# Convolution and two expert layers: single products in two units, and some of the tap sums moved to a DMA queue or to TensorE

## The chip, the cores and the metric

The kernel runs on one core of a Trainium2 chip. The metric is the time of one execution on the device in microseconds (us). An engine of the core has a queue of its own and works through it in order: TensorE (PE, with its weight loads as PEld), VectorE (DVE), ScalarE (ACT), GpSimd (POOL) and SyncE (SP, which only issues DMAs here). They wait for each other by semaphores.

## What is computed

`x` is 2 x 4096 x 192 and `weight_gen` 2 x 4096 x 8 x 7, all in float32. Three stages follow each other:

```python
w = exp(weight_gen - max)                      # softmax over the 7 taps of each of 8 heads
w = w / (sum(w) + 1e-9)
out[s, h, g] = sum_k w[s, h, k] * x_pad[s + k, h, g]      # causal convolution, 24 columns a head
y = square(relu(out @ w_in1)) @ w_out1         # 8192 x 192 -> 2048 -> 192
h = y @ w_in2
z = (h * clip(h + 3, 0, 6) / 6) @ w_out2
```

## The kernel before

**Tiles.** The 8192 tokens are cut into 16 blocks of 512 (each partition holds 64 consecutive tokens, a block takes four of each). 2048 hidden columns are taken 256 at a time: one *step* is one block with one such group (`FG` = 2), so there are 8 steps a block and layer and 256 in all. Each float32 factor of a product is split into a high and a low part, and a product is the sum of high x high, low x high and high x low.

**A step.** A step has a first product A (`make_A`, L313 `half`: 18 matmuls of half the array's height, two at a time, from `sh`, the high part of the block's x, and `sl`, the low part), then `relu` on ACT (L402), `square` on ACT or `gate` on DVE, the high part `gh` on either (L422), the low part `gl` on DVE (L428), and three steps later (`LAG`) a second product B, which adds into the bank `acc`. From step 6 on (`APART`), `emit_pair` weaves A of step i with B of step i - 3 in half-height matmuls. Both halves of the array add into one bank; they take turns, and `done` and `after` (L358 to L364) order that by an empty instruction on POOL (`nc.gpsimd.nop()`, L363) that waits for the last matmul of one half and that the first matmul of the other half waits for. The first six A and three B are emitted singly, B at full height (L377).

**Order of the steps.** Block 0's and block 1's steps alternate after the first one (`woven`), then block 2 and so on. Layer 2's first step is step 64.

**The convolution.** Of blocks 0 and 1 (`convolve_pe`) the products of tap and x are made on DVE, of block 0 taps 5 and 1 on POOL, joined there by one addition (L744); PE adds them into a bank by matmuls with the identity (L751, four records a tap). Copies (L249, L250), transposes (L266), high casts (L271) and low differences (L275) make `sh` and `sl`. The other blocks (`convolve`) have seven products (L675) and six additions (L689) on DVE, then a transpose on DVE (`turn`, L290), a way through DRAM and `split_hi`, `split_lo`. `softmax` makes the tap weights.

**The weights.** Group g of layer m comes by four DMAs of SP (`load_weights`, L91 and L97) and is split on DVE and ACT (`w_q` to `r_low`, L119 to L165). All eight groups of layer 1 are loaded in the opening. Layer 2's first load waits for the staging tiles `st`, which block 0's and block 1's tap products use before.

**Who sets the order.** The program is a list of `Op`s with the time that each is thought to take, what it waits for, the buffers it takes, and a due time (`due`, `at_step`). A loop at the end starts at each moment and on each engine the ready operation that is due first, and the instructions are emitted in that order, so each engine's queue has the order of that plan. On the chip an instruction waits for its semaphores only; what stands behind it in its queue waits too. `spin` fills PE with idle matmuls before the first step.

## Time and profile before

| | us |
|---|---|
| median of 3 runs | 1092.02 (1090.76 to 1092.54) |
| profiled execution | 1091.92 |
| its span (first to last instruction) | 1090.1 |
| mean granted clock of PE | 0.998 |
| busy in the span: PE, PEld | 1081.4, 940.7 |
| DVE, ACT, POOL | 923.2, 608.7, 8.8 |

The profile is of one execution; its times are counted from the first instruction. A busy PE is not PE at its peak, since the ends of matmuls are modelled and they overlap; holes are better seen from the starts of its weight loads. A step of the paired stage appears as L313, both for A (`h<-`) and for B (`acc<-`).

### The profile page before, as it was taken

What the parts mean: (1) busy time and instruction counts of PE and PEld (TensorE: products, weight loads), DVE (VectorE), ACT (ScalarE), POOL (GpSimd) and SP (SyncE); (2) the same over time, 40 slices, a digit from 0 to 9 for tenths busy, and PEclk for the clock granted to TensorE, in tenths of its full rate; (3) what the DMA queues carried; (4) which work ended last, traced back from release to release, by engine and by line L of the source; (5) the groups of instructions that cost most, each with busy time, mean ns of one, the idle gap of its engine ahead of it and who ended that gap; (6) DMA issues with size and microseconds to landing.
All of it is one profiled execution on the core that took longest, in us unless ns stands there. A gap on an engine that the chain in (4) does not pass through costs nothing.

```text
span 1090.1 us, 23712 instructions
## 1 busy us (share of the span) xinstructions
PE 1081.4 (99%) x9786; PEld 940.7 (86%) x9786; DVE 923.2 (85%) x1003; ACT 608.7 (56%) x662; POOL 8.8 (1%) x16
## 2 busy tenths in 40 slices
PE   8999999999999999999999999999999999999998
PEld 5788888888888888888888888888888888888887
DVE  7999999999999999999797676766757888888876
ACT  4999888889746556463544535454353333333322
POOL 2000000000000000000000000000000000000000
PEclk9999999999999999999999999999999999999999
DMA  9704351544310623222221112212032222133101
GB/s 224 184 16 123 79 166 51 165 117 102 114 39 16 191 59 86 93 71 59 73 74 45 56 48 74 59 44 69 25 79 59 69 69 69 46 82 83 30 28 47
DMA packets 67508, 86.73 MB, mean 80 GB/s; under 512 B 5516, under 2 KB 43532, under 8 KB 66504
## 3 DMA queue, kind: packets, MB, share of 16 engines
q1 hardware_dynamic: 67256, 85.01, 29.3%
q8 instruction: 77, 1.26, 0.5%
q14 instruction: 31, 0.25, 0.1%
q10 hardware_dynamic: 144, 0.20, 0.0%
HBM read 59.10 MB, written 26.08 MB: 78 GB/s over the span
## 4 chain that ended last, share of the span: by engine, by line
PE 95%; DMA 3%; DVE 1%; SPq 1%; ACT 0%; issue 0%; ACTq 0%
PE acc L313 49%; PE h L313 45%; DMA st<-in_moe_w_in_dram 2%; PE acc L377 1%; DMA wc<-in_weight_gen_dram 0%; DMA xc<-in_x_dram 0%; SPq L91 0%; SPq L97 0%; DVE hb L143 0%; DVE sl L275 0%; DVE t L132 0%; ACT g L402 0%; ACT g L406 0%; DVE q L158 0%; DVE w L165 0%
## 5 line engine op out<-in xcount | busy, mean ns | idle before, releaser
L313 PE MATMUL h<-sh,w 64*128 64x512 f32 x3072 | 521.2, 376 | 0.6 <-ACT g L402 0.5
L402 ACT ACTIVATE g<-h 128x1024 f32<-128x1024 f32 x256 | 262.6, 1026 | 456.4 <-PE h L313 435.7
L313 PE MATMUL acc<-gh,w 64*128 64x512 f32 x3000 | 511.7, 376 | 0.0
L313 PEld LDWEIGHTS h<-sh,w 64*128 64x128 f32 x3072 | 382.0, 186 | 43.3 <-ACT g L402 1.4
L313 PEld LDWEIGHTS acc<-gh,w 64*128 64x128 f32 x3000 | 375.3, 186 | 39.7
L313 PE MATMUL h<-sl,w 64*128 64x512 f32 x1536 | 355.7, 376 | 0.0
L313 PE MATMUL acc<-gl,w 64*128 64x512 f32 x2000 | 349.9, 376 | 0.0
L428 DVE TENSOR_TENSOR gl<-g,gh 128x1024 fp32r<-128x1024 f32 x256 | 312.5, 1221 | 19.3 <-ACT gh L422 12.7
L313 PEld LDWEIGHTS acc<-gl,w 64*128 64x128 f32 x2000 | 235.0, 186 | 26.5
L313 PEld LDWEIGHTS h<-sl,w 64*128 64x128 f32 x1536 | 236.9, 186 | 20.2
L410 DVE SCALAR_TENSOR_TENSOR g<-g,h 128x1024 f32<-128x1024 f32 x128 | 156.1, 1220 | 55.6 <-ACT g L402 54.8
L406 ACT ACTIVATE g<-g 128x1024 f32<-128x1024 f32 x128 | 135.7, 1060 | 1.2
L422 DVE CAST gh<-g 128x1024 fp32r<-128x1024 f32 x141 | 96.9, 687 | 42.2 <-PE acc L313 42.1
L422 ACT CAST gh<-g 128x1024 fp32r<-128x1024 f32 x115 | 119.7, 1041 | 2.6 <-DVE g L410 2.6
L675 DVE TENSOR_TENSOR pr<-xc,wc 128x768 f32<-128x768 f32 x84 | 79.8, 955 | 3.6 <-DMA xs<-aT 2.6
L689 DVE TENSOR_TENSOR a<-a,pr 128x768 f32<-128x768 f32 x84 | 80.0, 952 | 0.2
L235 DVE TENSOR_TENSOR sl<-x,sh 128x1536 fp32r<-128x1536 f32 x30 | 52.6, 1753 | 8.0 <-ACT sh L229 8.0
L229 ACT CAST sh<-x 128x1536 fp32r<-128x1536 f32 x25 | 36.8, 1471 | 0.1
L440 DVE TENSOR_SCALAR z<-acc 128x512 f32<-128x512 f32 x26 | 17.8, 684 | 16.6 <-PE acc L313 16.6
L129 ACT COPY t<-st 128x768 uint16<-128x768 uint16 x16 | 19.0, 1187 | 8.0 <-DMA st<-in_moe_w_out_dram 8.0
L751 PE MATMUL acc<-pp,ident 128*128 128x384 f32 x52 | 19.5, 531 | 1.9 <-DVE pp L740 1.8
L438 ACT ACTIVATE z<-acc 128x512 f32<-128x512 f32 x36 | 20.7, 599 | 0.0
(67 smaller groups left out, 298.0 us busy)
## 6 DMA issues: line engine op xcount, KB each, us to landing
x<-ys SPq DMA_DIRECT2D x32, 512.0 KB, 6.3
x<-xs SPq DMA_DIRECT2D x28, 384.0 KB, 5.2
xc<-in_x_dram SPq DMA_DIRECT2D x7, 1344.0 KB, 5.8
ys<-z SPq DMA_DIRECT2D x32, 256.0 KB, 2.1
st<-in_moe_w_in_dram SPq DMA_DIRECT2D x32, 192.0 KB, 6.1
zq<-zs SPq DMA_DIRECT2D x60, 96.0 KB, 2.4
out_dram<-o SPq DMA_DIRECT2D x15, 384.0 KB, 2.3
xs<-aT SPq DMA_DIRECT2D x56, 96.0 KB, 3.4
```

Source lines behind the costliest of these rows:

```text
L229: copy_on(engine)(xs_in[m, b][0], xraw[m, b][:, 0:NK])
L235: nc.vector.tensor_tensor(out=lo, in0=src, in1=hi.bitcast(F32), op=ALU.subtract)
L313: return lambda: nc.tensor.matmul(ps, w[r], turns(x[r]), start=start, stop=stop)
L402: nc.scalar.activation(g, ps, AF.Relu, bias=3.0 if m else 0.0)
L406: nc.scalar.activation(g, g, AF.Square)
L410: nc.vector.scalar_tensor_tensor(out=g, in0=g, scalar=6.0, in1=h_ps[m, b, f], op0=ALU.min, op1=ALU.mult)
L422: copy_on(engine)(gh, g)
L428: nc.vector.tensor_tensor(out=gl, in0=g, in1=gh.bitcast(F32), op=ALU.subtract)
L438: nc.scalar.activation(dst, src, AF.Copy, scale=scale)
L675: nc.vector.tensor_tensor(out=dst, in0=xs, in1=ws.to_broadcast([P, TB, H, G]), op=ALU.mult)
L689: nc.vector.tensor_tensor(out=total(), in0=total(), in1=prods.pop((b, k)), op=ALU.add)
L751: nc.tensor.matmul(attn[b][a][:, 0:2 * D], ident, v[:, a * 2 * D:(a + 1) * 2 * D], start=start, stop=stop)
```

## The change

- **Loads.** Block 1's softmax weights are loaded ahead of the expert weights (`load_w_rest`), apart from the rest of x.
- **Single products.** The first six A and three B are put in the plan as two operations each, a high unit (`emit_part(A, B, False)`: for A 12 of the 18 matmuls, for B 6 of 10) and a low unit, each waiting only for the parts that it reads.
- **Block 0.** POOL's addition of taps 5 and 1 is gone (`JOINED` is empty); PE adds seven taps.
- **Block 1.** After DVE has made taps 6, 5, 4 and 3 in two tiles of two, one DMA issued by POOL adds the tile (4, 3) to the tile (6, 5) (`gather`, 768 KB). PE adds five tiles in the order 2, 1, 0, 6, 5.
- **Block 2.** DVE makes taps 3, 2, 1 and 0 first, in two tiles; two DMAs on POOL's queue, one after the other, add the tile (1, 0) to (3, 2) and then 2 to 3; DVE makes taps 6, 5 and 4, adds these and at the end what the DMAs have made. The tiles are the staging tiles `st`, so that layer 2's first weights now wait for block 2.
- **The plan.** A DMA on POOL counts 1.0 us there and lands 5.0 us later (`LANDS`); DVE and POOL are taken not to run beside each other where both use a shared port (`port`); due times from step 2 on are 3 us later (`LATER`); a POOL product counts 1.5 us.

The diff, cut to its core:

```diff
+    def load_w_rest():
+        nc.sync.dma_start(out=wc[0][:, TB:, :], in_=w_v[:, TB:CT, :])
...
+    def emit_part(A, B, low):
+        if A:
+            if not low:
+                singles[A] = make_A(*A)
+            n = 2 * NK
+            for ops in zip(*[s[n:] if low else s[:n] for s in singles[A]]):
+                for op in ops:
+                    op()
+            return
+        m, b, f = B
+        if f == 0 and not low:
+            accs[m, b] = acc_tiles()
+        parts = g_sb.pop((m, b, f)) if low else g_sb[m, b, f]
+        first, last = f == 0, f + 2 == NF
+        for o in range(2):
+            for i in range(FG):
+                wh, wl, whl = w_out_of(m, f + i)
+                g = parts[int(low)][:, i]
+                for n, w in enumerate([whl] if o else [wh] if low else [wh, wl]):
+                    nc.tensor.matmul(
+                        accs[m, b][o], w, turns(g), start=(first and not low and i == n == 0),
+                        stop=(last and low and i == FG - 1),
+                    )
...
-    LATER = 0.0
+    LATER = 3.0
-    JOINED = [[(5, 1, "POOL")], []]
+    JOINED = [[], []]
-    POOLED = 1.8
-    ORDER = [(6, 4, 3, 2, 0, 5), range(K - 1, -1, -1)]
+    POOLED = 1.5
+    PSUMW = (0,)
+    SENT = (2,)
+    LANDS = 5.0
+    GATHERED = (1,)
+    ORDER = [(6, 4, 3, 5, 2, 1, 0), (2, 1, 0, 6, 5)]
...
+            self.port = "POOL" in times or list(times) == ["DVE"]
...
+    w_rest = first_load = add(None, load_w_rest, [(halos[-1], -99.0)], uses=both[1:], dmas=[(0.47, 0.3)])
...
+    def gather(out, in_):
+        flat = [v.rearrange("p n t h g -> p (n t h g)") if len(v.shape) == 5 else v for v in (out, in_)]
+        nc.gpsimd.dma_start(out=flat[0], in_=flat[1], accum_op=ALU.add)
+
+    def send(fn, deps, uses):
+        o = add({"POOL": 1.0}, fn, deps, uses=uses)
+        o.port = False
+        o.lands = LANDS
+        return o
...
+            o, made = None, {}
+            for n in range(2):
+                for i in range(2):
+                    o = add(
+                        cost, lambda n=n, i=i: mul2(n, i), [o] if o else deps, [("st", ("pp", b, n))], keys
+                    )
+            st = [("st", ("pp", b, n)) for n in range(2)]
+            s1 = send(lambda: gather(pairs[0], pairs[1]), [o], st)
+            s2 = send(lambda: gather(pairs[0][:, 0:1], pairs[0][:, 1:2]), [s1], st[:1])
+            o = a = add(cost, lambda: mul(K - 1), [o], [("a", b)], keys)
+            for k in (K - 2, K - 3):
+                o = add(cost, lambda k=k: mul(k), [o], [("pr", (b, k))], keys)
+                a = add(cost, lambda k=k: summed(k), [o, a], uses=[("a", b), ("pr", (b, k))])
+            return add(
+                cost,
+                lambda: nc.vector.tensor_tensor(out=attn[b], in0=attn[b], in1=flat(pairs[0][:, 0]), op=ALU.add),
+                [a, s2], uses=st[:1] + [("a", b)],
+            )
...
+        if b in GATHERED:
+            (k, _), (l, _), (i, _), (j, _) = seq[:4]
+            made[k] = made[l] = send(
+                lambda: gather(pairs[room(k)], pairs[room(i)]), [made[j]], [room(k), room(i)]
+            )
+            sums = [k for k in sums if k not in (i, j)]
...
-    m2_load.deps.append((conv[TURNED - 1], -99.0))
+    m2_load.deps.append((conv[max(SENT, default=TURNED - 1)], -99.0))
...
+        if not (A and B):
+            h = add({"PE": 6.45 * SLOT}, lambda: emit_part(A, B, False), deps[0], takes, uses)
+            due(h, at_step(i if A else j + LAG))
+            step_ops.append(h)
+            low = "lowA" if A else "lowB"
+            more = [(before[low], -1.0)] if low in before else []
+            p = add({"PE": (slots - 6.45) * SLOT}, lambda: emit_part(A, B, True), deps[1] + [h] + more, uses=takes + uses)
+            before[low] = p
```

## Rows read from the trace of the kernel before

**Rows 1.** The page, costliest groups: DVE's high casts (busy, mean ns | idle before).

```profile
L422 DVE CAST gh<-g 128x1024 fp32r<-128x1024 f32 x141 | 96.9, 687 | 42.2 <-PE acc L313 42.1
```

**Rows 2.** Chain that ended last, in order of time: start us, us, what.

```profile
52.52 1.27 PE h L313 x9
...
1077.92 6.75 PE acc L377 x30
```

**Rows 3.** Timeline of PEld, the opening: start us, us, instruction, [idle before <-releaser].

```profile
19.69 0.30 PEld L751 LDWEIGHTS acc<-pp,ident 128*128 128x128 f32 x2 [2.00 <-DVE pp L740]
...
24.16 1.16 PEld L313 LDWEIGHTS h<-sh,w 64*128 64x128 f32 x12 [0.55 <-issue]
...
31.22 3.52 PEld L751 LDWEIGHTS acc<-pp,ident 128*128 128x128 f32 x12 [0.33 <-issue]
34.87 0.94 PEld L377 LDWEIGHTS acc<-gh,w 128*128 128x128 f32 x4
...
40.91 1.21 PEld L313 LDWEIGHTS h<-sh,w 64*128 64x128 f32 x12 [0.33 <-ACT sh L271]
...
42.75 1.31 PEld L313 LDWEIGHTS h<-sh,w 64*128 64x128 f32 x12
...
45.59 1.16 PEld L313 LDWEIGHTS h<-sh,w 64*128 64x128 f32 x12 [0.89 <-ACT g L402]
...
47.95 1.16 PEld L313 LDWEIGHTS h<-sh,w 64*128 64x128 f32 x12 [0.55 <-ACT g L402]
...
50.09 0.73 PEld L377 LDWEIGHTS acc<-gh,w 128*128 128x128 f32 x4 [0.33 <-ACT g L406]
...
52.45 0.73 PEld L313 LDWEIGHTS h<-sh,w 64*128 64x128 f32 x8 [0.33 <-ACT gh L422]
```

**Rows 4.** Stretches: us, busy (x count) of each engine, PEclk, DMA share, GB/s.

```profile
18.00:19.00 1.00, 0.00 (x0) 0.00 (x0) 1.00 (x3) 1.00 (x3) 0.00 (x0) 1.00 1.16 264
20.00:21.00 1.00, 1.00 (x3) 0.44 (x2) 1.00 (x2) 1.00 (x3) 0.00 (x0) 0.50 1.15 257
22.00:23.00 1.00, 1.00 (x3) 0.52 (x2) 1.00 (x2) 0.00 (x0) 0.00 (x0) 0.50 1.17 226
```

**Rows 5.** Stretches ahead of and behind the start of the paired stage.

```profile
core 0: us, PE busy (x) PEld busy (x) DVE busy (x) ACT busy (x) POOL busy (x), PEclk, DMA share, GB/s
11.00:52.45 41.45, 38.31 (x211) 27.07 (x210) 38.12 (x64) 31.94 (x49) 0.20 (x1) 0.96 0.92 220
52.45:76.00 23.55, 23.55 (x219) 20.69 (x220) 23.55 (x29) 21.77 (x26) 0.00 (x0) 1.00 0.00 1
```

**Rows 6.** Timeline: block 1's fourth tap on DVE, block 0's last high part on ACT.

```profile
23.08 0.95 DVE L740 TENSOR_TENSOR pp<-xc,wc 128x768 f32<-128x768 f32 x1
...
20.00 0.61 ACT L271 CAST sh<-xt 128x512 fp32r<-128x512 f32 x1
```

**Rows 7.** The page, DMA issues: count, KB each, median us from issue to landing.

```profile
xc<-in_x_dram SPq DMA_DIRECT2D x7, 1344.0 KB, 5.8
ys<-z SPq DMA_DIRECT2D x32, 256.0 KB, 2.1
st<-in_moe_w_in_dram SPq DMA_DIRECT2D x32, 192.0 KB, 6.1
```

**Rows 8.** Timeline: block 0's sums on PE, and its first copy on ACT.

```profile
6.59 8.01 PE L751 MATMUL acc<-pp,ident 128*128 128x384 f32 x24
...
15.54 0.46 ACT L249 COPY x<-acc 128x384 f32<-128x384 f32 x1
```

**Rows 9.** Timeline of DVE: block 2's sum is turned, its low part split off.

```profile
75.73 1.00 DVE L290 STREAM_TRANSPOSE aT<-a 128x768 f32<-128x768 f32 x1
...
88.96 1.76 DVE L235 TENSOR_TENSOR sl<-x,sh 128x1536 fp32r<-128x1536 f32 x1
```

**Rows 10.** Line L363 on POOL's queue (all, then near 59 us), and PE beside it.

```profile
L363 POOLq EVENT_SEMAPHORE  x998: 17/17/17, 54.9 to 1076.1; - x200
...
L363 POOLq EVENT_SEMAPHORE  x2: 17/17/17, 59.0 to 59.1; - x2
...
59.46 0.38 PE L313 MATMUL acc<-gh,w 64*128 64x512 f32 x1
```

More of the change, by code (lines that the diff above doesn't have):

```diff
@@ L623, in s1 @@
             box.append(whole[:, 0:n, :])
-            if t1 == TB:
-                for i, k in enumerate(k for k, engine in TAPS[0] if engine == "POOL"):
-                    factor[k] = whole[:, n:2 * n, i:i + 1]
+            for i, k in enumerate(k for k, engine in TAPS.get(t0 // TB, []) if engine == "POOL" and c == 0):
+                factor[t0 // TB, k] = whole[:, n + i // 2 * n:2 * n + i // 2 * n, i % 2:i % 2 + 1]
             nc.vector.tensor_reduce(out=box[0][:, :, 0:1], in_=e(), axis=AX.X, op=ALU.max)
@@ L659, in softmax @@
         o = add({"DVE": two(cols)}, s4, [o], uses=[st] + keys)
+        o.port = False
         o = add({"DVE": 0.2}, s5, [o], uses=[st])
         o = add({"DVE": 0.1 + 7e-3 * n}, s6, [o], uses=[st])
[L662 to L666 removed]
+        if c:
+            return add({"DVE": two(cols)}, s7, [o], uses=[st] + keys)
+        for k, engine in TAPS[t0 // TB]:
+            if engine == "POOL":
+                factors[t0 // TB, k] = add({"POOL": 0.28}, lambda k=k: s7_of(k), [o], uses=[st] + keys)
+        return add({"DVE": two(cols)}, s7, [o], [("h", "w")] if b in PSUMW else [], [st] + keys)
+    def gather(out, in_):
[3 more added lines that the diff above has]
+        o = add({"POOL": 1.0}, fn, deps, uses=uses)
+        o.port = False
+        o.lands = LANDS
+        return o
     def convolve(b, deps):
@@ L753, in total @@
                 )
-        made, before = {}, {}
+        made, before, pairs = {}, {}, {}
         for k, e in seq:
-            more = ([before[e]] if e in before else deps) + needs(b, k)
+            more = ([(before[e], -0.1)] if e in before else deps) + needs(b, k)
             if e == "POOL" and e not in before:
-                more = list(factors.values()) + needs(b, k)
+                more = [o for (c, _), o in factors.items() if c == b] + needs(b, k) + deps[1:]
             o = add(
-                {e: two(TB * D) if e == "DVE" else POOLED}, lambda k=k, e=e: term(k, e), more, [room(k)], keys + extra
+                {e: two(TB * D) if e == "DVE" else POOLED}, lambda k=k, e=e: term(k, e), more,
+                [room(k)] + ([room(seq[4][0])] if b in GATHERED and not made else []), keys + extra,
             )
+            o.port = e == "POOL" or b not in PSUMW
             made[k] = before[e] = o
+            if b == 1 and not first_tap:
+                first_tap.append(o)
         sums = [k for k, _ in seq if k != LAST[b]]
@@ L766, in convolve_pe @@
             made[k] = add(
-                {e: two(TB * D) if e == "DVE" else POOLED}, lambda k=k, l=l, e=e: joined(k, l, e), [made[k], made[l]],
+                {e: two(TB * D) if e == "DVE" else 1.2 * POOLED}, lambda k=k, l=l, e=e: joined(k, l, e), [made[k], made[l]],
                 uses=[room(k), room(l)],
@@ L868, in x_on_pe @@
             takes = splits if j == 0 else []
+            more = [(first_tap[0], -99.0)] if b == 0 and GATHERED and j == 0 else []
             t = {"ACT": act_t(N), "DVE": two(N)}
             hi_pe.append(
-                add(t, lambda e, j=j: split_pe_hi(b, j, e), turns_pe[j:j + 1] + hi_pe[:1], takes, [key] + splits)
+                add(t, lambda e, j=j: split_pe_hi(b, j, e), turns_pe[j:j + 1] + hi_pe[:1] + more, takes, [key] + splits)
             )
             lo_pe.append(add({"DVE": two(N)}, lambda j=j: split_pe_lo(b, j), hi_pe[-1:], uses=[key] + splits))
+            lo_pe[-1].port = False
         x_ready[0, b], x_hi[0, b] = lo_pe, hi_pe
@@ L924, in products @@
     def products(i, A, j, B):
[L925 removed]
+        deps, takes, uses = [[], []], [], []
         if A:
@@ L944, in products @@
         slots = (9 if A else 0) + (10 if B else 0) + (0 if A and B else 0.9)
-        p = add({"PE": slots * SLOT}, lambda: emit_pair(A, B), deps, takes, uses)
-        due(p, at_step(i if A else j + LAG))
+        if not (A and B):
[6 more added lines that the diff above has]
+            before[low] = p
+        else:
+            more = [(before.pop(k), -1.0) for k in ("lowA", "lowB") if k in before]
+            p = add({"PE": slots * SLOT}, lambda: emit_pair(A, B), deps[0] + deps[1] + more, takes, uses)
+            h = p
+        due(p, at_step(i if A else j + LAG) + (0 if h is p else 6.45 * SLOT))
         fixed[p] = at_step(i if A else j + LAG) + slots * SLOT
@@ L1004, in released @@
                 late = min(late, 0.2)
-            t = max(t, d.start + 1e-6, d.end + lag + late + (0.02 if same else HOP))
+            end = d.start + d.times["PE"] if same and "PE" in d.times else d.end
+            t = max(t, d.start + 1e-6, end + lag + late + (0.02 if same else HOP))
         return t
@@ L1057, in conv_moe_moe2_kernel @@
             best.start, best.engine = t, e
+            if best.port and ("POOL" in best.times or e == "DVE"):
+                port_free = t + best.times[e]
             free[e] = t + best.times[e]
```

81 lines of the change are left out of this document (48 added, 33 removed).

## Prediction

> **What bounds the kernel now.** The page comes first: by its table of busy times TensorE (PE) hardly rests. "Busy" hides small gaps, so I read the chain of waits next. From 52.52 us on it is L313 on PE over and over, until the last block of L377 at 1077.92 [rows 2]. So the 250 paired steps run back to back: (1077.92 - 52.45) / 250 = 4.10 us a step, and the change touches nothing in their products. The time is the moment at which the paired stage starts (52.45 us, the first L313 weight load after the last single product [rows 3]) plus a constant 1037.6 us, plus whatever the change breaks in the paired stage. What can be won lies in the first 52 us; what can be lost lies there too, and behind it.
>
> The opening is read from PE's weight loads in order of time [rows 3], because they show what follows what. PE adds two taps of block 1 from 19.69, runs step 0's first product (A0) at 24.16, two taps, A1, three taps from 31.22, two second products (B0, B1) with the transposes of block 1 between them, then A2 to A5 from 40.91 and B2 at 50.09. That is 52.45 - 19.69 = 32.76 us with few holes. Real waits for ScalarE (ACT) stand before A4 and A5: an A step without a wait takes 42.75 - 40.91 = 1.84 us, but A3 takes 2.84 until A4 and A4 takes 2.36 until A5, which makes 1.5 us of waiting. The gaps of 0.55 and 0.33 us where full-height matmuls (128 rows) and half-height ones (64 rows) follow each other are there at each change of kind.
> The clock is the other loss: 0.50 of full speed, the 1.2 GHz level, from 20 to 23 us, after PE had stood idle at 18 to 19 us [rows 4]. The first two sums took 24.16 - 19.69 = 4.47 us, where three later ones took 34.87 - 31.22 = 3.65, or 1.22 each; the slow clock costs about 2 us.
> VectorE (DVE) is nearly full too: 38.1 of 41.45 us before the paired stage and 23.55 of 23.55 in the next stretch [rows 5]. It decides the order in which things become ready, but PE itself is the bound.
>
> **The change, part by part.**
> *Four taps added on the queue.* Block 1's sums on PE fall from seven to five: -2 x 1.22 = -2.4 us of PE time that lies on the path. In their place an accumulating DMA of 768 KB goes out on GpSimd's (POOL's) queue when DVE has made the fourth tap. Before, the fourth tap ends at 23.08 + 0.95 = 24.0 us [rows 6]. The softmax of block 1 now gets its weights before the first expert weights and can run before them on DVE; I take the fourth tap at 22 us (20.5 to 24). Its transfer is not in the trace. A plain copy of its size lies between 256 KB in 2.1 us and 1344 KB in 5.8 us [rows 7], so 2.1 + 512 x 3.7 / 1088 = 3.8 us; if its target has to be read as well, 1536 KB by the same slope, 6.5 us. The engines are full at that time (share 1.16 [rows 4]) with the weight stream, whose own pieces of 192 KB take 6.1 us [rows 7]; doubling the part that grows with size gives 11 us as the upper end. I take 7, nearer to the pieces that ran in the same crowd, so the sums of the gathered pair can begin near 30 us (25 to 36). When must it be there? Before, block 1's last sum ends at 34.9, 17.6 us ahead of the paired stage; with a new start near 50.0 and 1.5 us of waits gone, it must end by 33.9 and the transfer be in by 31.5. Behind the waiting sum on PE stand the rest of the sums, the transposes, and all later products. By 30 it costs nothing; what covers it is A0, A1, the three other sums and B0. The weight stream is slowed by the same bytes, at most 786 KB / 220 GB/s = 3.6 us [rows 5]; what covers that is that DVE, full as it is, and not the queue sets when a weight group is ready, so I cost it at nothing; without that cover it would be the 3.6 us.
> *GpSimd's two taps by TensorE.* The join of the two on POOL goes, and PE adds a seventh tap to block 0: +1.22 us. PE is full there already, 24 matmuls from 6.59 to 14.60 [rows 8], so nothing had waited for the join and the sums now end near 15.8. ACT took up the first copy only at 15.54, behind a block-1 exponential [rows 8] that now comes earlier. So only about 0.4 of the 1.22 us reaches the path.
> *Order of block 1's sums.* They begin with tap 2, the fifth one made, no longer with tap 6. PE's first work after block 0's transposes is then A0's high half. It needs the three high parts, the last at 20.61 [rows 6]. With the 0.4 us, and with ACT perhaps putting these casts ahead of the next weights, I take 20.3 us (19.2 to 21.0) where PE had begun at 19.69: +0.6 us (-0.5 to +1.3). The idle stretch before it is as long as now, so I keep the slow clock; at full clock it would be -2 us.
> *Products singly in two units.* The nine single products become a high unit and a low unit, with no matmul more. The ACT waits before A4 and A5 can be filled by B units: -1.5 us (0 to -1.5), taken whole, since B2 alone is 50.09 to 52.45 = 2.36 us of such filling. A unit put between two of the other height costs a change and a change back, 0.55 + 0.33 = 0.88 us; I count one more such pair, +0.9 (0 to 2.6 for three).
> *Half of block 2's additions on the queue.* DVE makes 10 operations where it made 13, some 2.9 us less at 0.96 each. Block 2's sum is turned at 75.73 and split at 88.96 to 90.72, while its first product comes at 52.45 + 10 x 4.10 = 93.5 [rows 9]; block 2 isn't on the path and has some 3 us to spare, so the gain is nothing by itself. It keeps DVE from falling behind when the paired stage starts 2 us earlier. Its two gathers run one after the other in the paired stage, with the final DVE addition waiting for the second and the low parts of g queued behind that addition. The transfers meet a nearly idle queue there (share 0.00 [rows 5]).
> *What the gathers pass on POOL's queue.* In the paired stage POOL carries 998 relay instructions (L363), four a step: PE may add into a bank with one half of the array only after POOL has seen the other half finish [rows 10]. A relay at 59.0 stands ahead of a sum that starts at 59.46, so POOL may be some 0.45 us late. Each gather waits in that queue for its taps, or for the transfer before it, with the relays behind it. The plan allows 1.0 + 5.0 us for a transfer; mine alone needs 3.8 to 6.5. I take the stall as 0; the ends are 0 and 5 us (a landing of 11 us).
> The sum: -2.4 + 0.6 - 1.5 + 0.9 = -2.4 us; the paired stage starts at 50.0. The profiled execution took 1091.92 us, 0.1 below the median of 1092.02, so the forecast is **1089.5 us**. A measurement of this kernel tells about 0.2% from no change, or 2.2 us, so this stands just beyond that bound.
>
> **Two rules weighed against rows.** DVE casts 1024 columns in 687 ns (L422, 0.67 ns each) [rows 1], while a tap of two operands takes 0.95 us for 768, or 1.24 ns each [rows 6]: it has a faster mode, in use 141 times. The Trainium skill, "SBUF — State Buffer", section "SBUF: two separate sides", says that such operations lock GpSimd out of a shared port, so that it cannot write the descriptors of a DMA that it issues. By that rule each gather would start up to 0.69 us later, and two late relays would cost 2 x (0.69 - 0.45) = 0.5 us, so the sum would be 1090.0 with it and is 1089.5 without. No run here shows it, since POOL issued no DMA.
> The weight stream keeps the engines' share at 1.16 while the gather runs [rows 4]. The same skill, "DMA: Bandwidth & Descriptors", section "Issuing engines are not separate DMA queues", says that transfers from all issuing engines interleave on the same 16. By that rule the gather takes longer than a lone copy's 3.8 us, which the end of 11 us holds; the sum is the same by both as long as the landing comes before 31.5 us, and what it is later than that is the first rival below.
>
> **Rivals.**
> *The gather is late (0.17).* If it lands at 33 to 35 us, block 1's last two sums wait 1.5 to 3.5 us and the gain is gone: 1091 to 1093 us. For it: the full engines, and a target read twice. Against it: 9 us between the fourth tap and 31.5.
> *PE keeps its clock (0.13).* If units and taps come soon enough, the slow stretch at 20 to 23 us shrinks: up to -2 us more, 1087.5 us. Against it: PE waits for the same high parts as now.
> *The relays are held up (0.12), slower than before.* A gather of block 2 stands in POOL's queue until its condition comes, PE runs out after 0.45 us, and every paired step behind it moves. It ends slower by over 2.2 us if the two waits cost PE over 2.4 + 2.2 = 4.6 us together, so from about 2.7 us of waiting each; with a landing of 9 to 11 us instead of the planned 6 it gives 1094 to 1096 us. For it: DVE is full, so the taps may come after their planned time. Against it: the idle DMA queue there.
> *The units stay together.* If the order puts each low unit behind its high one, the 1.5 us and the 0.9 us both go: 1090.1 us. It lies inside the forecast's case.
>
> **How the numbers follow.** The forecast's case has 0.58, from 1087.5 to 1091.5 by its own bounds; a good half of it (0.36) lies below 1089.8. With the clock rival's 0.13 and 0.01 of the late gather, faster is 0.50. The rest of the forecast's case (0.22) and most of the late gather (0.15) make 0.37 for no difference; the relays with 0.12 and a very late gather with 0.01 make 0.13 for slower. The range runs from 1086.5, the clock rival with some waits gone, to 1094.0, where the relays begin to decide.
>
> **What would show it.** Right: the chain's first paired L313 near 50.0 us and 4.10 us a step after it; five groups of sums for block 1; no idle PE at L313 between 55 and 80 us. The gather: its wait at the sums of L751 and its landing before 31.5. Wrong: a paired stage that starts at 52 us or later, PE waiting for POOL's relays, or steps longer than 4.10 us while block 2's gathers are out.

## The result and the profile after

The changed kernel takes **1102.93 us** (median of 5 runs, 1101.43 to 1104.43) where the kernel before takes 1092.02 beside it: ratio 1.0104 (95% interval 1.0091 to 1.0116). It is slower by 10.9 us, where 1089.5 and a range up to 1094.0 were forecast. The profiled execution took 1103.95 us with a span of 1102.2, so 12.1 us of span are to be found. In the changed kernel L315 is `half`, L365 the relay (the empty instruction on POOL between the two halves), L388 B in units, L454 `gl`, L703 `gather`, L761 block 2's last addition, L823 and L834 the products and sums of the taps; in the kernels of the experiments they lie a few lines further down.

The chain of waits of the changed kernel, in order of time (start us, us, what), answers to [rows 2]:

```profile
20.11 10.82 DMA pp<-pp
30.98 2.93 PE acc L834 x4
...
57.17 1.27 PE h L315 x9
...
70.36 6.27 DMA pp<-pp
...
90.41 1.55 PE h L315 x9
...
1089.05 6.69 PE acc L388 x30
```

Before, no DMA stood in this chain after 52.5 us. Now block 1's gather is in it, and one of block 2's in the middle of the paired stage. The relays on POOL's queue give the length of that stage; they answer to [rows 10]:

```profile
L365 POOLq EVENT_SEMAPHORE  x998: 17/17/17, 59.6 to 1087.2; - x200
```

From the first relay to the last it is 1027.7 us, before 1021.2. With the first paired weight load at 57.10 instead of 52.45 [rows 3] the 12.1 us of this one execution are: **start** +4.65, **paired stage** +6.5, **behind the last relay** +0.95 (1102.2 - 1087.2 = 15.0, before 14.0). The three have different causes.

**The opening.** Timeline of PEld (start us, us, instruction, [idle before <-releaser]):

```profile
21.78 2.23 PEld L834 LDWEIGHTS acc<-pp,ident 128*128 128x128 f32 x8 [0.33 <-issue]
...
25.40 0.94 PEld L834 LDWEIGHTS acc<-pp,ident 128*128 128x128 f32 x4 [0.33 <-issue]
30.98 0.50 PEld L834 LDWEIGHTS acc<-pp,ident 128*128 128x128 f32 x2 [4.63 <-DMA pp<-pp]
...
33.84 2.21 PEld L315 LDWEIGHTS h<-sh,w 64*128 64x128 f32 x12 [1.08 <-issue]
36.69 1.16 PEld L834 LDWEIGHTS acc<-pp,ident 128*128 128x128 f32 x4 [0.65 <-issue]
...
57.10 0.94 PEld L315 LDWEIGHTS h<-sh,w 64*128 64x128 f32 x9 [0.33 <-ACT q L126]
```

PE's loads end at 26.34 (25.40 + 0.94), and PE stands at tap 6's sum until the gather has landed, 4.63 us. A1 (33.84) and everything else stand behind that sum in its queue. Then it works slowly, as the stretches show (us, busy and count of each engine, PEclk, DMA share, GB/s; they answer to [rows 4]):

```profile
20.00:26.00 6.00, 5.71 (x27) 3.44 (x28) 6.00 (x10) 1.56 (x3) 1.01 (x1) 1.00 1.16 236
...
27.00:31.00 4.00, 0.02 (x1) 0.02 (x1) 3.15 (x7) 3.90 (x6) 0.00 (x0) 0.92 1.04 224
31.00:37.00 6.00, 6.00 (x17) 3.30 (x18) 3.28 (x5) 0.00 (x0) 0.00 (x0) 0.50 1.15 235
```

The granted clock is 1.00 at 20 to 26 us, where it was 0.50 before [rows 4]; after the 4.6 idle us it is 0.50, the 1.2 GHz level, for the 6 us from 31 to 37.

**The three gathers**, in the timeline of POOL and the shorter one in the list of DMA issues from 19 to 84 us (count, KB each, us from issue to landing):

```profile
20.11 1.01 POOL L703 DMA_DIRECT2D pp<-pp  x1 [10.96 <-DVE pp L823]
70.36 0.88 POOL L703 DMA_DIRECT2D pp<-pp  x1 [49.24 <-PE h L315]
76.93 0.85 POOL L703 DMA_DIRECT2D pp<-pp  x1 [5.68 <-DMA pp<-pp]
```

```profile
pp<-pp POOLq DMA_DIRECT2D x1, 384.0 KB, 5.4
```

**The paired stage.** The first gather of block 2 is issued at 70.36, and POOL came free for it with a product of PE (the relay ahead of it waited for that), not with a tap of DVE. In the timeline of DVE its four taps are there at 65.6, and what the late landing does is seen further down:

```profile
64.67 0.95 DVE L718 TENSOR_TENSOR pp<-xc,wc 128x768 f32<-128x768 f32 x1
...
82.40 0.96 DVE L761 TENSOR_TENSOR a<-a,pp 128x768 f32<-128x768 f32 x1 [4.11 <-DMA pp<-pp]
...
84.37 1.18 DVE L454 TENSOR_TENSOR gl<-g,gh 128x1024 fp32r<-128x1024 f32 x1
85.47 0.59 DVE L119 TENSOR_SCALAR q<-st 128x768 uint32<-128x768 uint32 x1
...
87.64 1.08 DVE L143 SCALAR_TENSOR_TENSOR hb<-st,q 128x768 uint32<-128x768 uint32 x1
```

DVE stands 4.1 us at block 2's last addition. Behind it in DVE's queue stand a low part of g (L454) and the split of layer 1's last weight group (L119, L143), whose high part ACT then writes (L152):

```profile
89.65 0.71 ACT L152 CAST w<-hb 128x640 fp32r<-128x640 f32 x1
```

PE needs both, and its timeline has three stops:

```profile
77.08 0.48 PE L315 MATMUL acc<-gh,w 64*128 64x512 f32 x1 [0.50 <-POOLq L365]
...
85.61 0.70 PE L315 MATMUL acc<-gl,w 64*128 64x512 f32 x4 [1.14 <-DVE gl L454]
...
90.41 1.55 PE L315 MATMUL h<-sh,w 64*128 64x512 f32 x9 [2.16 <-ACT w L152]
```

The relay that I had feared is the smallest of them; the largest is for the late weight group, the eighth to be split, which the paired step at 90.41 is the first to use. What they cost together is counted in stretches of 8 us (columns as above):

```profile
76.00:84.00 8.00, 7.50 (x70) 6.28 (x68) 3.89 (x6) 4.89 (x7) 0.85 (x1) 1.00 0.67 147
84.00:92.00 8.00, 4.70 (x40) 3.26 (x38) 7.96 (x12) 6.65 (x9) 0.00 (x0) 0.99 0.69 171
92.00:100.00 8.00, 8.00 (x62) 6.72 (x62) 6.25 (x8) 5.71 (x7) 0.00 (x0) 0.80 0.33 77
100.00:108.00 8.00, 8.00 (x78) 7.02 (x76) 7.74 (x8) 7.83 (x8) 0.00 (x0) 1.00 0.01 3
```

An undisturbed stretch has 78 matmuls; these have 8, 38 and 16 fewer, 62 x 8 / 78 = 6.4 us. The last 16 (1.6 us) go to the clock at 0.80 after the stops.

**The end.** Before the output's transposes PEld now stands 1.20 us:

```profile
1096.52 0.52 PEld L533 LDWEIGHTS ot<-x,z 128*128 128x128 f32 x4 [1.20 <-issue]
```

In the kernel before, the transposes (L507) followed the last product without a hole:

```profile
1084.28 0.63 PEld L507 LDWEIGHTS ot<-x,z 128*128 128x128 f32 x4
```

The last three B have no A either, so they too are emitted in units by `emit_part`, and the order `(1, 0)` that the old code kept for the very last step is lost: both output banks now finish at the end together.

### The profile page after: what moved, and what is told of

It reads as the page before. It is cut to its first block, busy times and chain, and to the rows that moved or that the text cites. A ratio compares the mean times of both kernels' runs of the same rounds, so it can differ in the third digit from the quotient of the medians.

```text
span 1102.2 us, 23709 instructions
## 1 busy us (share of the span) xinstructions
PE 1086.1 (99%) x9782; PEld 940.7 (85%) x9782; DVE 921.6 (84%) x1002; ACT 607.6 (55%) x660; POOL 9.7 (1%) x18
## 4 chain that ended last, share of the span: by engine, by line
PE 95%; DMA 3%; SPq 1%; ACT 0%; DVE 0%; issue 0%; DVEq 0%; POOLq 0%; ACTq 0%
PE acc L315 48%; PE h L315 45%; DMA pp<-pp 2%; PE acc L388 1%; DMA st<-in_moe_w_out_dram 1%; PE acc L834 0%; SPq L91 0%; DMA xc<-in_x_dram 0%; DVE pp L823 0%; SPq L97 0%; DVE gl L454 0%; PE ot L533 0%; ACT g L428 0%; ACT g L432 0%; ACT gh L448 0%
## 5 line engine op out<-in xcount | busy, mean ns | idle before, releaser
L315 PE MATMUL h<-sh,w 64*128 64x512 f32 x3072 | 524.5, 378 | 3.9 <-ACT w L152 2.2
L315 PE MATMUL acc<-gh,w 64*128 64x512 f32 x3000 | 512.5, 376 | 0.5 <-POOLq L365 0.5
L315 PEld LDWEIGHTS h<-sh,w 64*128 64x128 f32 x3072 | 383.2, 187 | 48.2 <-ACT w L152 2.6
L315 PEld LDWEIGHTS acc<-gh,w 64*128 64x128 f32 x3000 | 375.7, 186 | 40.8 <-POOLq L365 0.9
L315 PE MATMUL h<-sl,w 64*128 64x512 f32 x1536 | 357.3, 377 | 0.0
L315 PE MATMUL acc<-gl,w 64*128 64x512 f32 x2000 | 350.5, 377 | 1.1 <-DVE gl L454 1.1
L454 DVE TENSOR_TENSOR gl<-g,gh 128x1024 fp32r<-128x1024 f32 x256 | 312.3, 1220 | 21.7 <-ACT gh L448 15.1
L315 PEld LDWEIGHTS acc<-gl,w 64*128 64x128 f32 x2000 | 235.2, 186 | 28.1 <-DVE gl L454 1.5
L315 PEld LDWEIGHTS h<-sl,w 64*128 64x128 f32 x1536 | 237.4, 186 | 22.1 <-issue 1.2
L718 DVE TENSOR_TENSOR pr<-xc,wc 128x768 f32<-128x768 f32 x80 | 75.9, 953 | 3.4 <-DMA xs<-aT 2.5
L732 DVE TENSOR_TENSOR a<-a,pr 128x768 f32<-128x768 f32 x80 | 76.0, 950 | 0.2
L834 PE MATMUL acc<-pp,ident 128*128 128x384 f32 x48 | 18.4, 533 | 4.1 <-DMA pp<-pp 4.0
```

What stands on the lines that cost most here:

```text
L315: return lambda: nc.tensor.matmul(ps, w[r], turns(x[r]), start=start, stop=stop)
L454: nc.vector.tensor_tensor(out=gl, in0=g, in1=gh.bitcast(F32), op=ALU.subtract)
L718: nc.vector.tensor_tensor(out=dst, in0=xs, in1=ws.to_broadcast([P, TB, H, G]), op=ALU.mult)
L732: nc.vector.tensor_tensor(out=total(), in0=total(), in1=prods.pop((b, k)), op=ALU.add)
```

## The experiments

All 15 runs in one table; their edits and expectations follow. "Start" is the first paired weight load on PEld, "loss" the stretch from first to last relay less the 1021.2 us of before. Each ratio is to the kernel before run on the same chip.

| run | start us | loss us | median us | ratio |
|---|---|---|---|---|
| before | 52.45 | 0 | 1090.5 to 1092.0 | 1 |
| after | 57.10 | 6.5 | 1102.93 | 1.0104 (1.0091 to 1.0116) |
| e1 | 49.07 | 0.0 | 1090.20 | 0.9991 (0.9981 to 1.0000) |
| e2 | 55.76 | 2.8 | 1098.88 | 1.0075 (1.0058 to 1.0091) |
| e3 | 50.22 | 2.9 | 1092.12 | 1.0012 (1.0002 to 1.0021) |
| e4 | 52.84 | 1.1 | 1092.07 | 1.0014 (1.0004 to 1.0023) |
| e5 | 49.31 | 1.5 | 1090.31 | 0.9993 (0.9982 to 1.0003) |
| e6 | 56.62 | 5.9 | 1100.41 | 1.0080 (1.0065 to 1.0095) |
| e7 | 50.92 | 8.4 | 1099.73 | 1.0076 (1.0063 to 1.0089) |
| e8 | 48.70 | 4.1 | 1092.45 | 1.0012 (1.0003 to 1.0021) |
| e9 | 49.0 + 8.0 | 0.3 | 1097.87 | 1.0058 (1.0045 to 1.0071) |
| e10 | 54.85 | 1.1 | 1097.97 | 1.0064 (1.0049 to 1.0078) |
| e11 | 49.29 | 0.0 | 1088.90 | 0.9979 (0.9970 to 0.9988) |
| e12 | 49.53 | 3.7 | 1092.92 | 1.0018 (1.0009 to 1.0027) |
| e13 | 51.86 | 0.9 | 1092.06 | 1.0013 (1.0004 to 1.0021) |
| e14 | 50.23 | 0.2 | 1089.78 | 0.9992 (0.9983 to 1.0001) |
| e15 | 48.60 | 0.5 | 1088.75 | 0.9981 (0.9972 to 0.9990) |

Start, loss and the end add up to the profiled times, as they must, since all three are read from the same trace: for e1 they give 1091.92 - 3.38 + 0.0 + 0.8 = 1089.3, and its profiled execution took 1089.41. Start and loss are of one execution each. It lay 2.5 us above the median in e6, 2.2 in e4, 1.1 in e3 and 1.6 below it in e10, so a difference of about 1 us between two starts or losses says little by itself.

Against what was expected before each run, the median fell in the theory's range in e3, e4, e10, e11 and e15 (in e3 by chance, an earlier start against a loss that was not expected), and e9 followed its rival, 0.1 us below the rival's range. The others missed: e1 by 0.8 us to the good, e6 by 3.4, e7 by 5.7, e8 by 0.5 and e13 by 0.1 to the bad; e2 and e14 fell between theory and rival, e12 above both, and e5 came out as its rival said.

### Which gather costs what: e1, e2, e3

e1 takes out block 1's gather, with `ORDER` of its sums as without one (PE adds all seven taps, 6 first), e2 block 2's gathers, e3 both:

```diff
-    GATHERED = (1,)
-    ORDER = [(6, 4, 3, 5, 2, 1, 0), (2, 1, 0, 6, 5)]
+    GATHERED = ()
+    ORDER = [(6, 4, 3, 5, 2, 1, 0), range(K - 1, -1, -1)]
```

```diff
-    SENT = (2,)
+    SENT = ()
```

> Block 1's taps are added by TensorE again (seven sums, 6 to 0), all else as changed. Theory: block 1's gather lands 10.8 us after its issue where the plan has 6.0, TensorE waits 4.6 us for it and then runs at half clock to 37 us; and the late TensorE in turn holds block 2's gather behind the relays on GpSimd's queue, so that block 2's last addition stops VectorE for 4.1 us. Then without block 1's gather both losses go: the paired stage starts at 52 to 53 us, its steps keep 4.10 us to within 1 us in all, time 1091 to 1093.5. Rival 1 (block 2's gathers cost what they cost by themselves): the paired stage starts at 52 to 53 us but loses some 7 us between 75 and 95 us again, time 1098 to 1100. Rival 2 (the two units or the seventh tap are what costs): the start stays near 57 us, time 1101 to 1103.

> Block 2's additions are all on VectorE again, block 1's gather stays. Theory and rival 1: the paired stage starts near 57 us as in the changed kernel and then keeps 4.10 us a step, so only the 4.7 us of the opening are left: 1095.5 to 1097.5. Rival 2: the same start, and 1101 or more if the steps still lose.

> No DMA on GpSimd's queue at all: only the two units, the early softmax weights and the seventh tap are left of the change. Theory: the start is at 51 to 53 us and the steps keep 4.10 us, 1090.5 to 1092.5. Rival 1: the same. Rival 2: a start near 57 us and 1096 or more.

PEld's first paired weight load of e1:

```profile
49.07 0.94 PEld L315 LDWEIGHTS h<-sh,w 64*128 64x128 f32 x9 [0.33 <-issue]
```

Without block 1's gather the paired stage starts at 49.07, 8.0 us earlier than with it, although PE adds two taps more. (With the gather goes a rule of the plan that hangs on `GATHERED`: block 0's first high cast is not put ahead of block 1's first tap. e14 below keeps it and starts at 50.23.) And the paired stage loses nothing then: block 2's gathers go out at 54.13 and 62.25, and DVE waits 0.7 us at the last addition. So block 1's gather brought both large losses: its own in the opening, and the other because the plan made with it puts block 2's first gather behind the relays of three steps, where e1's plan puts it behind those of one.

Without block 2's gathers the paired stage loses 2.9 us in e3 and 2.8 in e2. In both PE waits for `gl` (0.66 and 0.51 us) and for the high part of the last weight group (0.17 and 1.76 us, ACT L152). e3 against e1 says what block 2's additions cost DVE there: 2.9 us by the profiles, 1.9 by the medians. That it is the early start that leaves no room for them is not shown: e2 starts 5.5 us later than e3 and loses the same, and the kernel before has all of these additions on DVE and loses nothing. `LATER` was 3.0 in every run of the changed plan, so whether it puts that weight group too late is open. e2 also shows the late gather alone: its 768 KB took 10.0 us, PE waited 4.7, start 55.76.

### What the plan believes: e4

`send` takes the landing as an argument: 10.0 us for block 1's gather, 5.7 for block 2's, instead of 5.0.

```diff
-    def send(fn, deps, uses):
+    def send(fn, deps, uses, lands):
...
-        o.lands = LANDS
+        o.lands = lands
```

> The same instructions as the changed kernel, but the plan counts 10.0 us for block 1's gather and 5.7 us for each of block 2's, close to what they took. Theory: TensorE's queue then has other products ahead of the sums that wait and block 2's gathers stand where their taps are done; the wait at the sums falls under 2 us, the start comes at 52 to 55 us, VectorE waits under 1 us for block 2, time 1091 to 1095. Rival 1: the start improves but VectorE still waits for block 2, 1096 to 1100. A third view, that the gather's bytes slow the weight stream and that this sets the time: no better than 1100.

Timeline of PEld: A1, B0's high unit and the gathered sums.

```profile
29.65 1.16 PEld L315 LDWEIGHTS h<-sh,w 64*128 64x128 f32 x12 [0.86 <-ACT w L152]
...
31.79 1.16 PEld L388 LDWEIGHTS acc<-gh,w 128*128 128x128 f32 x6 [0.33 <-issue]
32.98 2.34 PEld L834 LDWEIGHTS acc<-pp,ident 128*128 128x128 f32 x8
```

The gather takes as long as in the changed kernel (10.8 us), yet PE no longer waits for it, and the start is 52.84, 4.3 us better: with a landing close to the true one the plan puts A1 and B0 ahead of tap 6's sum. So it is less the duration than the plan's belief in 6 us (1.0 + 5.0) that costs. The paired stage gains too, with a loss of 1.1 us instead of 6.5: in this plan 8 relays stand ahead of block 2's first gather, not 12, and DVE waits 2.3 us instead of 4.1.

### The clock: e6

21 groups of idle matmuls before tap 6's sum, into columns of a bank that nothing reads (42 weight loads on the trace):

```diff
+            if b == 1 and k == K - 1:
+                for _ in range(21):
+                    nc.tensor.matmul(attn[b][0][:, 2 * D:2 * D + P], ident, ident, start=False, stop=False)
```

> The changed kernel with 21 idle matmuls on TensorE right ahead of the sum that waits for block 1's gather, so that TensorE works while the transfer is out (some 4.5 us). Theory: of the 7 us that the late gather costs the opening, 3 to 3.5 come from the half clock of 30 to 37 us; the wait of TensorE for the transfer goes to the idle matmuls, the two sums and the product behind them run at full clock, the paired stage starts at 53.5 to 54.5 us, block 2's gather is held for less long, time 1094 to 1097. Rival (the wait alone is the loss): the start stays at 56.5 to 57.5 us, time 1101 to 1104.

Timeline of PE, then stretches:

```profile
28.86 4.85 PE L835 MATMUL acc<-ident 128*128 128x128 f32 x42
33.55 1.46 PE L837 MATMUL acc<-pp,ident 128*128 128x384 f32 x4
```

```profile
29.00:37.00 8.00, 8.00 (x61) 6.62 (x60) 5.09 (x7) 3.97 (x6) 0.00 (x0) 1.00 1.15 228
```

The clock stays at 1.00, and from tap 6's sum to the paired stage it takes 56.62 - 33.55 = 23.1 us where the changed kernel took 57.10 - 30.98 = 26.1: the slow clock is worth some 3.0 us, which is also what 6 us at 0.50 lose. But the gather landed at 31.95 in this run (11.8 us after its issue) and the idle matmuls ended at 33.7, since the clock was 0.66 at 20 to 25 us and they began late; the kernel won only 2.5 us by the medians. Of the 8.0 us between e1's start and the changed kernel's, 4.6 are the wait and some 3.0 the clock. The two sums that PE has less (2.4 us) do not show, and that was not taken apart.

### The crowd: e7

The weight groups from the third on are loaded only when block 1's gather has landed:

```diff
+            if (m, g) == (0, 2):
+                depend(load, gathered[0])
...
+    lds[0, 2].deps.append((sent[0], 0.0))
```

> The changed kernel, but the loads of weight group 2 and all later ones wait until block 1's gather has landed, so that its transfer meets an almost empty queue. Theory (crowding): the gather lands about 6.3 us after its issue, as block 2's of the same size did, TensorE's wait at the sums goes to under 1 us, the paired stage starts by 52.5 us unless the weights are now late, block 2's gathers are not held, time 1090 to 1094. Rival (an accumulating transfer of this size takes 10 us in the opening whatever else runs): it lands 10 us after its issue, the start is 57 us or later, 1101 or more.

The chain within the first 30 us, then the timeline of DVE:

```profile
20.07 6.51 DMA pp<-pp
```

```profile
76.09 0.96 DVE L767 TENSOR_TENSOR a<-a,pp 128x768 f32<-128x768 f32 x1 [3.71 <-DMA pp<-pp]
76.97 0.82 DVE L168 SCALAR_TENSOR_TENSOR w<-t,q 128x640 fp32r<-128x640 uint32 x1
```

Alone the same gather takes 6.5 us instead of 10.8, so 4.3 of it is the weight stream beside it. The start comes at 50.92. The paired stage then loses 8.4 us, so this is no cure: block 2's first gather is late here too (its taps are there at 59.6, it goes out at 64.29 behind 12 relays), DVE waits 3.7 us at the last addition (L767), and the weight part for which PE's loads wait 5.3 us (L168) stands behind that addition. How much of it the paused loads add is not shown.

### Why block 2's gathers are late: e9 and e10

e9 is e1 with 74 more matmuls before the first paired step, whose results the step's first product overwrites: PE is then 8 us late, as in the changed kernel.

```diff
+        if A == steps[APART]:
+            for op in late[A] * 37:
+                op()
```

> As e1_no_gather_block1 (which loses nothing in the paired stage), with 37 extra pairs of matmuls ahead of the first paired step whose result is overwritten: TensorE is 37 x 0.216 = 8.0 us late against the plan and nothing else changes. Theory (a late TensorE holds block 2's gathers, which stand behind its relays on GpSimd's queue, and so stops VectorE at block 2's last addition): VectorE waits 3 us or more there and the paired stage loses 3 to 6 us on top of the 8.0, time 1101 to 1104. Rival (a late TensorE only gives the others more time): no more than the 8.0 us, 1098 to 1099.

The loss beyond the 8 us is 0.3 and DVE waits 1.1 us: in e1's plan, where 4 relays stand ahead of the first gather, a late PE alone does not block DVE. The next suspect is POOL's queue. There `emit_pair` emits all four relays of a step at once, so a gather that the plan puts inside a step stands behind the relays of the whole step. The plan that the changed kernel works out has it 0.6 us into a step, and in POOL's queue 12 relays, three whole steps, stand ahead of it instead of 8. e10 is the changed kernel with the gathers emitted among the step's instructions, where the plan has them:

```diff
-        for ops in zip(*seqs):
+        for n, ops in enumerate(zip(*seqs)):
+            if (A, B) in pauses and n == pauses[A, B][0]:
+                for o in pauses.pop((A, B))[1]:
+                    emit(o, o.engine)
...
+                    if order[i] in sent:
+                        moved += order[n:i + 1]
+                        pauses[pair_of[o]] = int((order[i].start - o.start) / SLOT), order[n:i + 1]
+                        break
```

> The changed kernel with the same plan, but a gather that the plan starts within a paired step is put among that step's instructions at its planned place; before, all four relays of the step stood ahead of it on GpSimd's queue (12 relays ahead of block 2's first gather, now 8). e9 spoke against a late TensorE as the cause; the new theory is that a gather waits for the end of the step in which the plan starts it: in the plan it starts at 57.8 us, 0.6 us into the step of 57.2, so it is held some 3.7 us, and VectorE's wait of 4.1 us for block 2's last addition is that hold. Theory: block 2's first gather is issued some 4 us earlier relative to the start of the paired stage (8.8 us after it in place of 13.3), VectorE waits under 1 us at L761, the paired stage loses 1 to 2.5 us in place of 6.5, time 1097 to 1099.5, with the opening as late as in the changed kernel. Rival (the transfers themselves are too long for the plan): VectorE still waits 3 us or more, 1101 to 1104.

Timelines of POOL and DVE, and the relays:

```profile
64.01 0.87 POOL L707 DMA_DIRECT2D pp<-pp  x1 [43.19 <-DVE q L158]
```

```profile
76.29 0.96 DVE L768 TENSOR_TENSOR a<-a,pp 128x768 f32<-128x768 f32 x1 [0.19 <-DMA pp<-pp]
```

```profile
L366 POOLq EVENT_SEMAPHORE  x998: 17/17/17, 57.3 to 1079.6; - x200
```

The first gather now goes out 9.2 us after the start (64.01 - 54.85) instead of 13.3 and follows DVE, which waits 0.2 us at the last addition instead of 4.1, and the stage loses 1.1 us instead of 6.5. That is the cause of most of the second loss. (This execution also started 2.2 us earlier than the changed kernel's, which the edit does not explain; the medians differ by 5.0 us, near the 5.4 of the loss.) What is left above before (1.0064) is the opening.

### The end, and the best of it: e5, e11

e5 is e1 with the last step emitted whole; e11 is e5 with the gathers inside the step:

```diff
-        if not (A and B):
+        if not (A and B) and B != steps[-1]:
```

> As e1_no_gather_block1, but the last step's second product is again one piece with its second output first. In e1 its two outputs both end with the last matmuls and 1.20 us pass between the last L388 weight load group and the last turning of the output, where the kernel before had none. Theory: the split of the last step costs 0.9 us of the tail in every version of the change, so this takes 1.0 us less than e1: near 1089.3, and faster than before by 1 to 2 us. Rival (the tail has another cause): the same as e1, 1090.2.

> As e5_last_step_whole (no gather for block 1, last step whole), with block 2's gathers put among the step's instructions as in e10. In e1 and e5 the holds are by the plan 0.7 and 2.8 us. Theory: VectorE's last wait for block 2 goes, the paired stage starts near 49.3 us and loses under 0.5 us, time 1088.5 to 1089.8, faster than before by 1 to 2.5 us. Rival (the holds of e5 cost nothing, its loss is chance): the same as e5, 1090.3.

In e5 PEld has no hole before the output's transposes:

```profile
1082.67 0.63 PEld L533 LDWEIGHTS ot<-x,z 128*128 128x128 f32 x4
```

From the last relay to the end it takes 14.2 us where e1 takes 14.8, so 0.6 us come back. e5's time does not show it: its second gather went out 13.2 us after the start, as e1's did (62.49 - 49.31 and 62.25 - 49.07), but took 6.7 us where e1's took 5.2, and DVE waited 2.3 us. In e11 block 2's first gather and the relays stand so:

```profile
53.53 1.00 POOL L707 DMA_DIRECT2D pp<-pp  x1 [44.10 <-PE acc L315]
```

```profile
L366 POOLq EVENT_SEMAPHORE  x998: 17/17/17, 51.8 to 1073.0; - x200
```

The second gather follows at 59.73, DVE does not wait for it, and nothing is lost in the paired stage. **1088.9 us** (0.9979) beats both kernels, the one before by 0.2%.

### What makes the early start: e8, e12, e13, e15

e8 is e1 and e15 is e11, both with all single products whole as before, the last ones too. e12 is e5 with POOL's join of taps 5 and 1 put back (`JOINED`, and tap 1 out of `ORDER[0]`). e13 is e11 with block 1's softmax weights loaded behind the first expert weights again.

```diff
-        if not (A and B):
+        if False:
...
-                early = (0.0, 0.0)
+                early = (0.0, 0.8)
```

```diff
-    JOINED = [[], []]
+    JOINED = [[(5, 1, "POOL")], []]
```

```diff
-    w_rest = first_load = add(None, load_w_rest, [(halos[-1], -99.0)], uses=both[1:], dmas=[(0.47, 0.3)])
+    first_load = halos[-1]
...
+                w_rest = add(None, load_w_rest, [(ld, -99.0)], uses=[("wc", 0)], dmas=[(0.47, 0.5)])
```

> As e1_no_gather_block1, but every single product is one operation again, as before the change. Theory (the units fill the waits for ScalarE in front of A4 and A5, 1.5 us, and let A0's high half start early): the paired stage starts 1.5 to 2.5 us later than e1's 49.2, at 50.7 to 51.7 us, the last step ends 0.9 us earlier, time 1090.5 to 1092. Rival (the early softmax and block 1's earlier taps give e1 its start): the start stays near 49.2, time 1089 to 1089.8.

> As e5_last_step_whole, but GpSimd adds block 0's taps 5 and 1 again and TensorE sums six tiles. Theory: the seventh sum costs 1.22 us of TensorE, of which 0.4 us or less reach the path, so this takes 0 to 0.5 us less than e5: 1089.8 to 1090.3. Rival (the join on GpSimd had been the last tile to come, so the seventh sum gains): 0.5 to 1.5 us more than e5.

> As e11_best_guess, but block 1's softmax weights are loaded behind the first expert weights again, as before the change. Theory (the early softmax, which lets block 1's taps start at 16 us in place of 18.7, gives the early start): the paired stage starts 1.5 to 3 us later than e11's 49.4, time 1090.2 to 1092. Rival (the other order of the plan gives it): the start stays within 0.7 us of e11's, time 1088.6 to 1089.8.

> As e11_best_guess, but every single product is one operation, as before the change. Theory (the units are worth nothing here; e8 lost 4.1 us in its paired stage to held gathers): the start is within 0.7 us of e11's 49.4, time 1088.3 to 1089.6. Rival (the units let the parts be made in a better order for VectorE): 1 us or more slower than e11, with the loss in the paired stage.

PEld's first paired weight load, first of e13, then of e15:

```profile
51.86 0.94 PEld L315 LDWEIGHTS h<-sh,w 64*128 64x128 f32 x9 [0.33 <-issue]
```

```profile
48.60 0.94 PEld L315 LDWEIGHTS h<-sh,w 64*128 64x128 f32 x9 [0.33 <-ACT gh L452]
```

With the late softmax weights the start moves from 49.29 to 51.86, and most of the gain of the opening is gone: the early start is theirs for the most part. In e11 four of block 1's sums are done before A0 (22.86 us), in e13 two. Whole single products start 0.7 us earlier than the units (48.60) and the time is the same (1088.75 to 1088.90, ratios 0.9981 and 0.9979): the units win nothing here. The seventh sum of block 0 costs nothing that shows: e12, with six sums, starts at 49.53, e5 with seven at 49.31. The times of e8 and e12 are above e1's and e5's because their paired stages lose 4.1 and 3.7 us (their first gathers go out at 57.87 and 58.69, and DVE waits 3.7 and 2.4 us at the last addition), so only their starts are compared.

### Does block 1's gather pay if planned right: e14

The whole change with 10.0 us for block 1's landing in the plan, gathers inside the step and the last step whole.

> The whole change with all mends: the plan counts 10.0 us for block 1's gather, block 2's gathers stand inside their step, the last step is whole. Theory (the transfer comes too late whatever the plan does, since block 1's x waits for it): the paired stage starts at 52 to 53.5 us as in e4, loses under 0.7 us, time 1091 to 1093, slower than e11 by 2 to 4 us. Rival (with nothing held, two sums less on TensorE do pay): 1088 to 1089.5.

Timeline of PEld:

```profile
26.89 1.16 PEld L315 LDWEIGHTS h<-sh,w 64*128 64x128 f32 x12 [0.86 <-ACT w L152]
...
29.34 1.16 PEld L389 LDWEIGHTS acc<-gh,w 128*128 128x128 f32 x6 [0.64 <-DVE gh L452]
30.53 2.34 PEld L841 LDWEIGHTS acc<-pp,ident 128*128 128x128 f32 x8
```

A1 and B0's high unit now stand before the gathered sums (30.53), PE's longest stop from A0 on is 0.9 us, and 1089.78 (0.9992) is 13 us below the changed kernel. The gather is then no gain: the paired stage starts at 50.23, 0.9 us after e11's, and the time is 0.9 us longer, which the two intervals can't tell from none.

## Why the prediction was wrong

**The frame held.** In e1 and e11 the paired stage takes the 1021.2 us of before whatever its start, so undisturbed steps still take 4.10 us; what the forecast had at nothing is the loss in that stage. The forecast's own start of 50.0 was reached without the gather (e11: 49.29), but by chance: e11 has none of the -2.4 us of two sums fewer.

**"I take 7 ... By 30 it costs nothing; what covers it is A0, A1, the three other sums and B0"** is the step that failed. The fourth tap came early (19.5 us instead of 22), and the transfer took 10.8 us, my upper end, so that it landed at 30.93, inside the 31.5 that I had set. PE stood 4.6 us all the same. The cover was counted by the clock and not by the queue: the plan held the landing for 6 us after the issue, 26.1, and so had put A1 and B0 behind the gathered sums. I had read the plan's 1.0 + 5.0 us and used it for block 2 alone. e4 and e14 show it: as long a transfer (10.8 and 10.3 us), other order, no stop at the sums. The crowd that I weighed is real: the same transfer took 10.8 us beside the weight stream and 6.5 without it (e7). With that the trace agrees with the Trainium skill, "DMA: Bandwidth & Descriptors", section "Issuing engines are not separate DMA queues", by which transfers of all issuing engines interleave on the same 16 DMA engines.

**The rival of the late gather (0.17)** had the right place, but its condition, a landing at 33 to 35 us, did not come, and its price of 1091 to 1093 us was too small. It counted the wait alone: the clock's 3.0 us (e6) and the loss that the moved steps bring to block 2 were not in it. **That PE keeps its clock** at 20 to 23 us came true in the profiled execution (1.00; in e6, with the same opening up to there, it was 0.66), and the clock fell later, in a hole that the change itself made.

**"I take the stall as 0"** for POOL's queue was nearly right for what I meant, 0.5 us, and wrong for what happened. I looked at relays behind a gather. The gathers stood behind relays: four a step, emitted at once, 4.7 us from ready taps (65.6) to issue (70.36), plus 6.3 and 5.4 us of transfer. The paired stage lost 6.5 us, where this term stood at nothing; 5.4 of them are that hold (e10). **"The low parts of g queued behind that addition"** was named and costed at nothing; of PE's stops 1.14 us came that way, and 2.16 by the last weight group, which the forecast did not name. e9 speaks against the late start as the cause, e10 shows the hold. My rival of held-up relays that ends slower had another mechanism and 1094 to 1096 us.

**Block 2's additions "the gain is nothing by itself"**: this can't be said of the changed plan, where taking them back to DVE costs 1.9 us (e3 against e1, medians). "It keeps DVE from falling behind when the paired stage starts 2 us earlier" is not shown as the reason, since e2 starts late and loses as much.

**The units, -1.5 us for filled ACT waits and +0.9 for one change of height**: e15 has neither and the same time as e11. The sum of -0.6 can't be told from nothing, and the -1.5 alone did not come. What moved the start was the load of the softmax weights, 2.6 us by e13, which I had used only to move a tap. **The seventh sum at 0.4 us** did not show: without it (e12) the start was 0.2 us later.

**The end was not looked at.** "The nine single products" are those of the opening; the last three B go through the same branch, and 0.6 to 0.9 us of the result is theirs.

**The two rules.** POOL's DMA instruction took 0.85 to 1.02 us for 31 of the 35 gathers in these traces. For the other four it took 1.08 to 1.42 us: there a DVE operation of one input, in the faster mode, had begun meanwhile and was still running at the usual end, and POOL's instruction ended 0.09 to 0.13 us behind it. In e1, timelines of POOL and DVE:

```profile
54.13 1.42 POOL L703 DMA_DIRECT2D pp<-pp  x1 [44.83 <-DVE w L165]
```

```profile
54.74 0.72 DVE L119 TENSOR_SCALAR q<-st 128x768 uint32<-128x768 uint32 x1
```

With that the traces agree with the Trainium skill, "SBUF — State Buffer", section "SBUF: two separate sides", by which such an operation keeps GpSimd from writing the descriptors of a DMA that it issues. No run varied it on purpose. It cost up to 0.4 us a gather, where the forecast allowed 0.69, and none of the losses above needs it.

**The 12 us together.** They are about 4.6 of waiting and 3.0 of clock in the opening, against a start that would be 3.4 us earlier, then 6.5 in the paired stage and 1 at the end.

## What to carry to other kernels

Where a plan orders in-order queues, a wait is covered by what the plan has put ahead of the waiter, and that follows from the duration that it believes, not from slack in time: give it the transfer's time as measured beside its neighbours before judging the transfer. A DMA issued from a queue that also carries synchronisation waits for all that is emitted ahead of it, so emit it where it is meant to go and not behind a whole step's relays. And when a branch is changed for the opening, look who else takes it: here the last steps did.

## What the runs showed of the hardware

- The accumulating DMA of 768 KB from SBUF to SBUF took 10.0 to 11.8 us beside the weight stream (share 1.10 to 1.12 while it ran; the longest in e6) and 5.9 to 7.2 us where hardly anything else moved (share 0.57 to 0.67; the longest in e13).
- The one of 384 KB took 5.2 to 7.1 us, but beside layer 2's first weight loads, which go out when the first gather lands (share 0.73 to 0.88). So the two sizes can't be compared here.
- After a hole of 4.6 us on PE (26.3 to 31.0) the granted clock was 0.50, the 1.2 GHz level, from 31 to 37 us with PE busy throughout. With idle matmuls in the hole it stayed at 1.00, 2.4 GHz, from 29 to 37 us (e6).
